# Transposes of the second row tile after a quarter of the first Q tile, and a shorter filler ahead of it

## The chip, the cores and the metric

The kernel runs on one core of a Trainium2 chip. The metric is the time of one execution in device microseconds (us). A profile also gives the span, from the first to the last instruction on the core; it is some 1.7 to 1.9 us shorter than the time. Most tables here are in spans and in moments counted from the span's start, because the change moves a few tenths of a us at one place in the first 8 us.

## The reference

A layer normalization of x (2048 rows of 512), then two branches from the same normalized rows: sliding attention (32 heads of 16, window of 8 with dilation 2) and a gated GELU block of width 1376; the result is x plus both.

```python
x = A_x
xn = _layernorm(x, axis=-1)
return x + _A_ref(xn, A_wqkv, A_wo) + _B_ref(xn, B_w_gate, B_w_up, B_w_down)
# _A_ref begins with: qkv = x @ wqkv     (512 -> 3*512)
# _B_ref: h = gelu(x @ w_gate) * (x @ w_up); h @ w_down
```

What matters for the change is only how the work begins. Before TensorE can do the first product (Q of row tile 0, that is of the first 128 rows), x must land, be normalized by VectorE and ScalarE, be transposed by TensorE into PSUM, and be copied back to SBUF.

## The kernel before

The program is a list of tasks that a small scheduler orders by estimated durations and gives semaphores. The tasks of the start on TensorE (PE) are held in a fixed order by a chain:

```python
WARM = cfg.get("WARM", ([512] * 9 + [128], [512, 128, 128, 128, 128]))
# ... one matmul of ones per entry, to keep the PE busy while it has no data ("fillers")
return lambda e: e.matmul(PS[:, 512 * it.slot:512 * it.slot + wn], lhsT=one_l,
                          rhs=one_r[:, 0:wn], start=True, stop=True)
# ...
if t == 0 and which == 0:                       # Q of row tile 0 is cut in two
    t_mm = G.task("pe", "mma0_0", 8 * 0.0563, mk_mm((0, 1)), ...)    # 8 of its 16 matmuls
    gs = (2, 3)
t_mm = G.task("pe", "mmt%d_%d" % (which, t), 4 * len(gs) * 0.0563, mk_mm(gs), ...)
# ...
chain(warm_tasks[:len(WARM[0])] + ["tpx0_0"] + warm_tasks[len(WARM[0]):] +
      ["mma0_0", "tpx0_1", "mmt0_0", "mmt0_1", "mmt1_0", "tpx1_0", ...])
```

`tpx0_0` and `tpx0_1` are the transposes of row tiles 0 and 1, four matmuls each; `mma0_0` and `mmt0_0` the two parts of Q of tile 0; `mmt0_1` is Q of tile 1, the first that needs tile 1's transposed copy; `mmt1_0` is K of tile 0. The first group of ten fillers stands ahead of tile 0's transposes, the second group of five between them and the first Q matmuls. The fillers are there for PE's clock: its matmuls of 512 columns come 0.427 us apart at first and 0.216 later.

## Time and profile before

| | before |
|---|---|
| time, median of the first 3 runs | 194.46 us |
| span of the profiled run | 192.5 us |
| PE busy | 187.8 us (98%) |
| VectorE, ScalarE busy | 79%, 55% |
| chain that ended last | 95% PE |
| second tile's matmuls wait for the copy | 0.20 us, at 7.47 |

In such a kernel, time is to be had only where PE idles or does work that nobody needs. The fillers are such work, and the 0.20 us such idling; both lie in the first 8 us. The prediction shows the lines.

### The profile page before, as it was taken

Reading aid. Unit: us, or ns where it says so; the run is one execution under the profiler, and the core shown is the slowest. Engines: PE = TensorE matmul, PEld = TensorE weight load, DVE = VectorE, ACT = ScalarE, POOL = GpSimd, SP = SyncE. Lnnn points to the kernel's source line nnn. Section 1 sums busy time; section 2 is a strip of 40 time slices with the busy share of each in tenths; the row PEclk is TensorE's granted clock in tenths of the full one; section 3 lists DMA queues with packets and bytes.
Section 4 is the critical chain, followed back from the end, with each engine's and each line's share of the span. In section 5 each row is a group of like instructions: output and inputs, shape, how many; then the busy total and the mean of one; then the engine's idle time right before and its main releaser. Section 6 shows DMA issues by size and latency. Waiting matters only on the chain.

```text
span 192.5 us, 3287 instructions
## 1 busy us (share of the span) xinstructions
PE 187.8 (98%) x1244; PEld 92.8 (48%) x1260; DVE 151.7 (79%) x239; ACT 105.9 (55%) x176; POOL 15.6 (8%) x31
## 2 busy tenths in 40 slices
PE   8999999999999999999999999999999999999995
PEld 2894444444444444444444444444444444444484
DVE  5799998999999955999698598998996099912132
ACT  5688574686896766700667587338276720058000
POOL 6010011111931100000000000000000000000000
PEclk9999999999999999999999999999999999999999
DMA  4999998799554033984501497510240496130131
GB/s 141 354 393 329 314 183 167 184 280 207 126 127 109 0 90 85 242 190 110 163 0 50 115 243 170 131 64 0 68 144 9 110 232 160 46 112 0 37 87 44
DMA packets 34800, 27.04 MB, mean 140 GB/s; under 512 B 11264, under 2 KB 33248, under 8 KB 34784
## 3 DMA queue, kind: packets, MB, share of 16 engines
q1 hardware_dynamic: 34784, 26.83, 55.9%
q8 instruction: 10, 0.16, 0.3%
q14 instruction: 6, 0.05, 0.1%
HBM read 19.99 MB, written 5.26 MB: 131 GB/s over the span
## 4 chain that ended last, share of the span: by engine, by line
PE 95%; issue 1%; DMA 1%; DVE 0%; ACT 0%; SPq 0%; DVEq 0%
PE PS L1395 36%; PE PS L1474 20%; PE PS L1152 18%; PE PS L1470 7%; PE PS L1363 4%; PE PS L1098 4%; PE PS L1236 4%; PE PS L1430 2%; DMA XIN<-in_A_x_dram 1%; PE PS L1229 1%; PE PS L1040 1%; PE PS L870 0%; SPq L927 0%; DVE XIN L1014 0%; DVE OB L1494 0%
## 5 line engine op out<-in xcount | busy, mean ns | idle before, releaser
L1474 PE MATMUL PS<-Wd,HT 128*128 128x512 bf16 (+2 forms) x208 | 41.1, 345 | 0.1
L1412 ACT ACTIVATE UU<-PS 128x512 bf16<-128x512 f32 x40 | 24.2, 604 | 29.9 <-PE PS L1395 29.8
L1395 PE MATMUL PS<-xnT,Wu 128*128 128x512 bf16 x155 | 39.7, 379 | 0.6 <-issue 0.5
L1395 PE MATMUL PS<-xnT,Wg 128*128 128x512 bf16 x156 | 39.5, 379 | 0.5 <-issue 0.3
L1206 DVE TENSOR_TENSOR UNI<-QT,KT 128x2048 bf16<-128x2048 bf16 x32 | 37.1, 1218 | 2.6 <-PE PS L1363 2.5
L1152 PE MATMUL PS<-xnT,Wqkv 128*128 128x512 bf16 x157 | 35.2, 379 | 0.2
L1405 ACT ACTIVATE GG<-PS 128x512 bf16<-128x512 f32 x40 | 23.8, 602 | 18.9 <-PE PS L1395 15.9
L1417 DVE TENSOR_TENSOR HT<-GG,UU 128x512 bf16<-128x512 bf16 x40 | 16.4, 416 | 18.1 <-ACT UU L1412 18.0
L1474 PEld LDWEIGHTS PS<-Wd,HT 128*128 128x128 bf16 x209 | 19.6, 98 | 18.5
L1395 PEld LDWEIGHTS PS<-xnT,Wu 128*128 128x128 bf16 x160 | 15.4, 98 | 19.4 <-issue 1.3
L1395 PEld LDWEIGHTS PS<-xnT,Wg 128*128 128x128 bf16 x160 | 15.5, 98 | 19.3 <-issue 0.8
L1152 PEld LDWEIGHTS PS<-xnT,Wqkv 128*128 128x128 bf16 x160 | 15.6, 98 | 18.6
L1343 DVE TENSOR_TENSOR UNI<-BS,PT 128x2048 bf16<-128x2048 bf16 x16 | 19.5, 1221 | 1.9 <-DMA out_dram<-OB 1.8
L1343 DVE TENSOR_TENSOR BS<-BS,PT 128x2048 bf16<-128x2048 bf16 x16 | 19.6, 1224 | 0.4
L1494 DVE TENSOR_TENSOR OB<-PS,XR 128x512 bf16<-128x512 f32 (+2 forms) x19 | 11.4, 604 | 10.5 <-PE PS L1474 10.4
L1470 PE MATMUL PS<-Wo,OT 128*128 128x512 bf16 (+2 forms) x75 | 16.9, 345 | 0.1
L1176 ACT ACTIVATE VT<-PS 128x512 bf16<-128x512 f32 x16 | 9.6, 597 | 4.4 <-PE PS L1152 4.4
L944 DVE BATCH_NORM_STATS2 st<-XIN 128x6 f32<-128x512 bf16 x15 | 10.1, 685 | 1.2 <-DMA XIN<-in_A_x_dram 1.2
L1375 ACT ACTIVATE OT<-PS 128x512 bf16<-128x512 f32 x16 | 8.3, 603 | 5.0 <-PE PS L1363 5.0
L1470 PEld LDWEIGHTS PS<-Wo,OT 128*128 128x128 bf16 x76 | 7.2, 98 | 7.0
L1192 POOL COPY KT<-KT 128x64 bf16<-128x64 bf16 x3 | 7.9, 2639 | 15.2 <-ACT KT L1169 13.8
L1162 ACT ACTIVATE QT<-PS 128x512 bf16<-128x512 f32 x12 | 7.2, 597 | 3.1 <-PE PS L1152 3.1
(74 smaller groups left out, 153.0 us busy)
## 6 DMA issues: line engine op xcount, KB each, us to landing
BS<-vt_scratch SPq DMA_DIRECT2D x64, 128.5 KB, 3.5
vt_scratch<-VT SPq DMA_DIRECT2D x16, 128.0 KB
XR<-in_A_x_dram SPq DMA_DIRECT2D x16, 128.0 KB, 3.4
out_dram<-OB SPq DMA_DIRECT2D x14, 128.0 KB, 1.7
Wqkv<-in_A_wqkv_dram SPq DMA_DIRECT2D x3, 512.0 KB
XIN<-in_A_x_dram SPq DMA_DIRECT2D x6, 256.0 KB, 4.3
Wg<-in_B_w_gate_dram SPq DMA_DIRECT2D x1, 1280.0 KB, 8.1
Wu<-in_B_w_up_dram SPq DMA_DIRECT2D x1, 1280.0 KB
```

The lines of the kernel that those rows point to most:

```text
L944: return lambda e: e.bn_stats(out=st[:, t, :], in_=XIN[:, it.slot, t2, :])
L1152: ins = e.matmul(PS[:, 512 * it.slot:512 * it.slot + HWD], lhsT=lhsT, rhs=xnT[:, itx.slot, kt, c0:c0 + HWD], start=(kt == 0), stop=(kt == 3))
L1176: return lambda e: e.activation(out=VT[:, ito.slot, 0:HWD], in_=PS[:, 512 * it.slot:512 * it.slot + HWD], func=ACTF.Identity)
L1206: return lambda e: e.tensor_tensor(out=UNI[:, it.slot, :, :], in0=bass.AP(QT, (itq.slot * 4 + g) * 512, [[NQT * 4 * 512, 128], [0, 4], [1, ...
L1343: return lambda e: e.tensor_tensor(out=dst(), in0=bass.AP(BS, it.slot * 4 * 514 + o, [[NBS * 4 * 514, 128], [514, 4], [128, 4], [1, 128]]) ...
L1395: ins = e.matmul(PS[0:M, 512 * it.slot:512 * it.slot + 512], lhsT=Wx[:, kt, j * 128:j * 128 + M], rhs=xnT[:, itx.slot, kt, :], start=(kt = ...
L1405: return lambda e: e.activation(out=GG[0:M, ito.slot, :], in_=PS[0:M, 512 * it.slot:512 * it.slot + 512], func=ACTF.Gelu_apprx_tanh)
L1412: return lambda e: e.activation(out=UU[0:M, ito.slot, :], in_=PS[0:M, 512 * it.slot:512 * it.slot + 512], func=ACTF.Identity)
L1417: return lambda e: e.tensor_tensor(out=HT[0:M, ito.slot, j, :], in0=GG[0:M, ig.slot, :], in1=UU[0:M, iu.slot, :], op=ALU.mult)
L1470: ins = e.matmul(PS[:, 512 * it.slot:512 * it.slot + CW], lhsT=OT[:, ito.slot, dq, ti * 128:(ti + 1) * 128], rhs=Wo[:, dq, c0:c1], start=( ...
L1474: ins = e.matmul(PS[:, 512 * it.slot:512 * it.slot + CW], lhsT=HT[:, ith.slot, j, ti * 128:(ti + 1) * 128], rhs=Wd[:, j, c0:c1], start=Fal ...
L1494: return lambda e: e.tensor_tensor(out=OB[:, ito.slot, 0:CW], in0=PS[:, 512 * it.slot:512 * it.slot + CW], in1=XR[:, itx.slot, c0:c1], op= ...
```

## The change

The intent is to bring tile 1's transposes, and so its copy, forward, so that the matmuls of tile 1 need not wait for it; and to take out filler that stands in front of the first Q matmuls. The durations that the scheduler plans with are kept, so the order of all other instructions stays.

```diff
-            def mk_w(it=it_warm, wn=wn):
-                return lambda e: e.matmul(PS[:, 512 * it.slot:512 * it.slot + wn], lhsT=one_l,
-                                          rhs=one_r[:, 0:wn], start=True, stop=True)
+            def mk_w(i=i, it=it_warm, wn=wn):
+                n = min(wn, 128) if i >= len(WARM[0]) else wn
+                return lambda e: e.matmul(PS[:, 512 * it.slot:512 * it.slot + n], lhsT=one_l,
+                                          rhs=one_r[:, 0:n], start=True, stop=True)
 ...
-                            t_mm = G.task("pe", "mma0_0", 8 * 0.0563, mk_mm((0, 1)), rd=mrd, wr=[it_mm],
+                            t_mm = G.task("pe", "mma0_0", 8 * 0.0563, mk_mm((0,)), rd=mrd, wr=[it_mm],
 ...
-                            gs = (2, 3)
-                        t_mm = G.task("pe", "mmt%d_%d" % (which, t), 4 * len(gs) * 0.0563, mk_mm(gs), rd=mrd,
+                            gs = (1, 2, 3)
+                        t_mm = G.task("pe", "mmt%d_%d" % (which, t), (8 if len(gs) == 3 else 16) * 0.0563, mk_mm(gs), rd=mrd,
```

Every line number from here on is one higher (L1098 becomes L1099).

## The prediction

> **What bounds the kernel now.** I read the page of the profile first, then the chain of waits cut to the first 20 us, then the timeline of 5 to 8 us, where the changed instructions stand. From the page, the busy table, the slices and the chain:
>
> ```profile
> PE 187.8 (98%) x1244; PEld 92.8 (48%) x1260; DVE 151.7 (79%) x239; ACT 105.9 (55%) x176; POOL 15.6 (8%) x31
> ...
> PE   8999999999999999999999999999999999999995
> ...
> PE 95%; issue 1%; DMA 1%; DVE 0%; ACT 0%; SPq 0%; DVEq 0%
> ```
>
> The reader is to see that TensorE (PE) is the engine at the limit from the first slice to the last, and that the chain that ended last is 95% PE. No other engine can give anything back except at the start, where the chain passes through DMA, VectorE and ScalarE. A tenth of a us taken from a PE gap at the start moves all that follows, if no fixed event (a load that lands when it lands) stands in the way.
>
> The timeline, at the place that is changed (start and length in us):
>
> ```profile
> 5.38 0.95 PE L870 MATMUL PS<-const-bfloat16-1.0 128*128 128x512 bf16 x5
> 5.63 0.38 ACT L1060 ACTIVATE xnT<-PS 128x256 bf16<-128x256 bf16 x1
> ...
> 6.02 0.35 DVE L1014 TENSOR_SCALAR XIN<-XS,rstd 128x512 bf16<-128x512 bf16 x1
> 6.11 0.49 PEld L1098 LDWEIGHTS PS<-xnT,Wqkv 128*128 128x128 bf16 x8
> 6.17 0.61 PE L1098 MATMUL PS<-xnT,Wqkv 128*128 128x128 bf16 x8
> ...
> 6.61 0.39 PE L1040 MATMUL PS<-ident,XIN 128*128 128x128 bf16 x4
> ...
> 6.83 2.60 PE L1098 MATMUL PS<-xnT,Wqkv 128*128 128x128 bf16 x40
> 7.04 0.38 ACT L1060 ACTIVATE xnT<-PS 128x256 bf16<-128x256 bf16 x1 [1.03 <-PE PS L1040]
> ...
> 7.47 1.79 PEld L1098 LDWEIGHTS PS<-xnT,Wqkv 128*128 128x128 bf16 x32 [0.20 <-ACT xnT L1060]
> ```
>
> L870 are the filler matmuls on a constant, L1040 the transposes of a row tile, L1060 the copy of the transposed tile out of PSUM, L1098 the Q and K matmuls. Order on PE: transposes of tile 0, fillers (one of 512 columns, four of 128), 8 Q matmuls of tile 0 (half of its 16), transposes of tile 1, the other 8, then 32 (Q of tile 1, K of tile 0), of which the first need tile 1's copy. The last line is the one that matters: PE stands idle because its next matmul needs tile 1's copy, which ends at 7.04 + 0.38 = 7.42. The 8 matmuls before it have run out at 7.28 (starts at 6.83, one each 0.0555 us), so 0.19 us of PE are lost there. The chain agrees: it goes through the PE queue, not through VectorE:
>
> ```profile
> 5.59 0.74 PE PS L870 x5
> 6.33 0.45 PE PS L1098 x8
> 6.78 0.22 PE PS L1040 x4
> 7.00 0.45 PE PS L1098 x8
> 7.45 0.03 issue
> 7.47 1.96 PE PS L1098 x32
> ```
>
> Tile 1's normalized row is ready at 6.02 + 0.35 = 6.37 (the DVE line), so its transposes, at 6.61, do not wait for data: they stand behind fillers and half a Q tile.
>
> **What the Trainium skill says.** "TensorE: Matmul & The Clock Gate", section "Wait — 56ns, not 53.3ns?", gives start-to-start times of 106.7 and 426.7 ns cold (128 and 512 columns) and 55.6 ns warm (128). The trace agrees: the 512-column filler takes 5.38 to 5.81, 0.43 us; eight Q matmuls go from 6.17 to 6.61, 0.055 us each. The same page, "What's actually happening", has the clock at half rate until a busy window of about 3.4 us has passed, the window not being tied to the kernel's start. Here the trace's clock record goes to full at 6.07 us, in the middle of the fillers, so the fillers are nearly all cold; the page's row of granted clock prints 9 from the start and does not show this. "Perfetto Trace Analysis", section "Tensor Engine Instruction (MATMUL, LD_WEIGHTS)", says that PE ends are estimated; I therefore use starts, and the pitch of 0.0555 us, never the printed 0.22 us of one matmul.
>
> **The change part by part.** The order of instructions on every engine is otherwise the same in both kernels (I compared the two built programs, waits included); the durations that the scheduler plans with were kept, so nothing else is rearranged. Two constants from the trace: a dependent weight load starts 0.05 us after its producer ends (7.42 to 7.47; also 4.92 to 4.97 for tile 0's transposes), and the copy starts 0.26 us after the start of the last transpose (6.78, one pitch before 6.83, to 7.04).
>
> (a) First filler 512 to 128 columns. Removes 0.43 - 0.107 = 0.32 us of filler: five cold ones end at 5.38 + 5 x 0.107 = 5.92. The Q matmuls cannot start there: tile 0's copy ends at 5.63 + 0.38 = 6.01, so the weight load goes at 6.06 and the matmul with it, against 6.17. Worth 0.11 us at that point; 0.14 us of PE idle take the place of the filler.
>
> (b) Four Q matmuls instead of eight ahead of tile 1's transposes. Removes 4 x 0.0555 = 0.22 us in front of them. With (a) the four are done at 6.06 + 0.01 + 4 x 0.0555 = 6.30 (0.01 for the first pair, as between the loads at 7.47 and 7.49). But tile 1 is ready only at 6.37, so the transposes start at 6.43: a new wait of about 0.13 us, and a gain of 6.61 - 6.43 = 0.18 us instead of 0.33.
>
> (c) The copy. Four transposes end at 6.43 + 0.01 + 0.22 = 6.66, the last starting at 6.61; copy from 6.87 to 7.25; the waiting load may go at 7.30, against 7.47.
>
> (d) The 12 matmuls that now stand between: 6.66 + 12 x 0.0555 = 7.33. That is after 7.30, so PE, not the copy, sets the start: the 0.19 us wait is gone, and the 32 matmuls start at 7.33 against 7.48.
>
> Sum: 0.15 us. As a balance of idle time: 0.19 saved at 7.28, 0.32 of filler saved, 0.14 + 0.13 of new waits and small parts given back.
>
> Each part alone, by the same steps: (b) alone has four matmuls from 6.17 to 6.39, the transposes still at 6.43, so the whole 0.15. (a) alone has eight from 6.06 to 6.52, so 0.09. In this reckoning the filler adds nothing once the split is in.
>
> Does 0.15 us reach the end? The next places: tile 2's transposes stand at 9.27 and need its normalization, which ends at 8.71 + 0.35 = 9.06. PE would come at 9.12, the data at 9.11 even unmoved, and the DVE chain that makes it hangs on tile 1's copies and so moves too. K weights are needed at 7.33 + 0.89 = 8.22 and have landed by 7.66, when the gate weights' load, which waits for them, is issued. The gate weights land 8.1 us later, at 15.8, and are used at 16.77. So nothing fixed is in the way. Later PE waits are of 0.2 to 0.4 us behind PE's own results or copies, which move with it. 194.46 - 0.15 = 194.31.
>
> **The rivals.**
> 1. Another wait takes the whole gain: the Q weights. The trace's semaphore updates have them landed at 5.79, 0.27 us before the new start at 6.06, so a late load would cost only the filler's part, and (b) would still get its 0.15. Time 194.3. Against total absorption, 194.46: the slack at tile 2 is thin (0.01 us if DVE does not move), but DVE does move.
> 2. ScalarE becomes the bound: the first Q copy waits for 12 matmuls instead of 8 after the transposes, and starts at 7.53 instead of 7.48, with the small square root of tile 2 behind it. That one also waits for statistics that now come earlier. At most 0.05 us is given back: 194.36.
> 3. The clock: the 0.14 us of idle falls into the window that ends at 6.07. It takes 4% from a window otherwise full of fillers, and a window that began before the fillers was evidently not enough. If that, or the loose phase of the window, kept the clock cold for one more window of 3.4 us, PE would lose 1.7 us: 196.2. The three runs of before are 0.14 us apart, so the phase hardly varies here; I give it 4%.
> 4. Small shifts of DMA and PSUM timing in the remaining 185 us go either way by 0.1 us or so; the spread of before (194.37 to 194.51) is as big as the gain.
>
> **Range and chances.** Middle 194.3. From rivals 2 and 4, 194.0 to 194.6 should hold it 8 times in 10, with the tail above from rival 3. Two per cent is 3.9 us, more than this stretch holds: faster by over 2% has 1%, slower 2%, the same 97%.
>
> **What would show it.** In the changed profile: Q matmuls from about 6.06 in a group of 4; transposes of tile 1 at 6.43 with a wait on VectorE in front of them (the step most likely wrong); copy at 6.87; no wait on ScalarE's copy at 7.3, or under 0.03 us; first gate matmul at 16.62 instead of 16.77; span 192.4. The prediction is wrong if filler or Q matmuls after 6.1 still come 0.107 us apart, if tile 2's transposes wait for VectorE by over 0.1 us, or if the gain at the first gate matmul is not there at the end.

## The result, and the profile after

| | before | after |
|---|---|---|
| median | 194.41 us (6 runs, 193.95 to 194.51) | 194.28 us (6 runs, 194.07 to 194.84) |
| ratio after / before | | 0.9999, 95% interval 0.9983 to 1.0015 |
| span of the profiled run | 192.5 | 192.4 |

A ratio is the mean time of one kernel's fast runs over that of the other's of the same rounds, so it is not quite the ratio of the medians. The measured median is 0.03 us from the predicted 194.31, and inside the range. But the ratio says that the gain of 0.15 us is smaller than what six runs resolve, so the mechanism has to be read from the traces.

The timeline of the changed kernel (start and length in us, engine, line, instruction, count; in brackets the idle time before it and what ended it):

```profile
5.34 0.51 PE L871 MATMUL PS<-const-bfloat16-1.0 128*128 128x128 bf16 x5
5.59 0.39 ACT L1061 ACTIVATE xnT<-PS 128x256 bf16<-128x256 bf16 x1
...
5.98 0.35 DVE L1015 TENSOR_SCALAR XIN<-XS,rstd 128x512 bf16<-128x512 bf16 x1
6.02 0.23 PEld L1099 LDWEIGHTS PS<-xnT,Wqkv 128*128 128x128 bf16 x4 [0.35 <-ACT xnT L1061]
6.03 0.40 PE L1099 MATMUL PS<-xnT,Wqkv 128*128 128x128 bf16 x4 [0.18 <-ACT xnT L1061]
6.39 0.23 PEld L1041 LDWEIGHTS PS<-ident,XIN 128*128 128x128 bf16 x4
6.39 0.40 PE L1041 MATMUL PS<-ident,XIN 128*128 128x128 bf16 x4
6.57 2.50 PEld L1099 LDWEIGHTS PS<-xnT,Wqkv 128*128 128x128 bf16 x44
6.63 2.62 PE L1099 MATMUL PS<-xnT,Wqkv 128*128 128x128 bf16 x44
6.83 0.39 ACT L1061 ACTIVATE xnT<-PS 128x256 bf16<-128x256 bf16 x1 [0.86 <-PE PS L1041]
```

The Q matmuls now wait for the copy of tile 0 (the bracket on L1099) and not for fillers. The transposes stand at 6.39, 0.05 us after tile 1's normalization (5.98 + 0.35 = 6.33). The 44 matmuls after them run in one piece from 6.63 on: the bracket with the wait for the copy, which stood at 7.47 before, is gone.

The chain of waits of the changed kernel at the same place:

```profile
5.59 0.39 ACT xnT L1061
5.98 0.05 issue
6.03 0.40 PE PS L1099 x4
6.42 0.37 PE PS L1041 x4
6.79 2.46 PE PS L1099 x44
9.25 0.22 PE PS L1041 x4
```

Before, this piece of the chain was all PE, with the fillers in it. Now it enters PE from ScalarE's copy, and L871 is no longer in it. The transposes of tile 2 follow at 9.25 against 9.44 before.

From there on nothing differs. Subtracting the moment of the first load of gate weights from the span leaves 175.99 us in the trace before (192.55 - 16.56) and 175.99 in the trace after (192.36 - 16.37). The gain of 0.19 us in the span all arises before 16.4 us, and all of it reaches the end. Of the 0.19, about 0.04 is not the change's: x landed that much earlier in this run (tile 0's normalization ends at 4.89 instead of 4.92). The rest, 0.15, is what the prediction had.

### The profile page after: what moved, and what is told of

Its sections match the earlier page's. It is cut to its first block, busy times and chain, and to the rows that moved or that the text cites. A ratio compares the mean times of both kernels' runs of the same rounds, so it can differ in the third digit from the quotient of the medians.

```text
span 192.4 us, 3303 instructions
## 1 busy us (share of the span) xinstructions
PE 189.0 (98%) x1260; PEld 92.6 (48%) x1260; DVE 151.8 (79%) x239; ACT 105.9 (55%) x176; POOL 15.7 (8%) x31
## 3 DMA queue, kind: packets, MB, share of 16 engines
HBM read 19.99 MB, written 5.26 MB: 131 GB/s over the span
## 4 chain that ended last, share of the span: by engine, by line
PE 96%; DMA 1%; ACT 1%; issue 0%; SPq 0%; DVE 0%; DVEq 0%
PE PS L1396 36%; PE PS L1475 20%; PE PS L1153 18%; PE PS L1471 7%; PE PS L1364 4%; PE PS L1099 4%; PE PS L1237 4%; PE PS L1431 2%; DMA XIN<-in_A_x_dram 1%; PE PS L1230 1%; ACT XR L955 1%; PE PS L1041 0%; SPq L928 0%; ACT xnT L1061 0%; ACT sq L976 0%
## 5 line engine op out<-in xcount | busy, mean ns | idle before, releaser
L1396 PE MATMUL PS<-xnT,Wu 128*128 128x512 bf16 x160 | 40.6, 379 | 0.0
L1396 PE MATMUL PS<-xnT,Wg 128*128 128x512 bf16 x160 | 40.3, 379 | 0.0
L1418 DVE TENSOR_TENSOR HT<-GG,UU 128x512 bf16<-128x512 bf16 x40 | 16.4, 417 | 18.0 <-ACT UU L1413 18.0
```

The source lines that it names most:

```text
L1396: ins = e.matmul(PS[0:M, 512 * it.slot:512 * it.slot + 512], lhsT=Wx[:, kt, j * 128:j * 128 + M], rhs=xnT[:, itx.slot, kt, :], start=(kt = ...
L1418: return lambda e: e.tensor_tensor(out=HT[0:M, ito.slot, j, :], in0=GG[0:M, ig.slot, :], in1=UU[0:M, iu.slot, :], op=ALU.mult)
```

## The experiments

All runs are of one core. By the rule of 2% the verdict of every run is "same", but for e10_lead5_wq_act, which is "unclear"; a run is called slower below where its whole interval lies above 1. Besides the times, each gave a trace. A table of all traces comes first: when the clock goes full (the trace's clock record; "none" where it has no such record), when the last part of the Q weights lands (semaphore updates in the trace), the end of tile 1's normalization, the start of its transposes, the weight load of the first matmul of tile 1 (the point where before had its wait), and the span minus the moment of the first gate weight load.

| run | clock full | Q weights | norm 1 | transposes 1 | first of tile 1 | span | rest |
|---|---|---|---|---|---|---|---|
| before | 6.07 | 5.79 | 6.38 | 6.61 | 7.47 | 192.55 | 175.99 |
| after | 5.45 | 5.56 | 6.34 | 6.39 | 7.26 | 192.36 | 175.99 |
| e1_split_only | 6.31 | 5.81 | 6.30 | 6.46 | 7.32 | 192.42 | 175.99 |
| e2_filler_only | 4.77 | 5.77 | 6.21 | 6.40 | 7.26 | 192.34 | 175.99 |
| e3_lead5 | 5.00 | 5.95 | 6.21 | 6.36 | 7.22 | 192.31 | 176.00 |
| e4_lead12 | 5.10 | 6.15 | 6.19 | 6.95 | 7.81 | 192.89 | 175.99 |
| e5_before_again | 5.64 | 6.55 | 6.35 | 7.13 | 7.99 | 193.10 | 175.99 |
| e7_fill_tiny | none | 5.99 | 6.18 | 6.34 | 7.20 | 192.30 | 175.99 |
| e8_warm_late | 9.72 | 6.19 | 6.30 | 6.71 | 8.31 | 194.10 | 175.98 |
| e9_lead0 | 6.46 | 5.90 | 6.42 | 6.57 | 7.63 | 192.74 | 175.99 |
| e10_lead5_wq_act | 12.88 | 5.26 | 8.57 | 8.77 | 10.26 | 196.62 | 175.98 |
| e11_after_third | 4.86 | 6.01 | 6.17 | 6.37 | 7.22 | 192.32 | 175.99 |
| e12_split_again | none | 5.83 | 6.14 | 6.20 | 7.07 | 192.16 | 175.99 |

The last column is the firmest finding: whatever happens in the first 16 to 21 us, the remaining part takes the same time to within 0.02 us.

Two more things stand in the traces. The clock record runs at full for 187.73 us in nine of them and for 184.32 in e8_warm_late and e10_lead5_wq_act, which is 55 and 54 times 3.413 us: the full clock comes and goes in steps of one such window. And the end of tile 1's normalization moves with the clock: it comes 1.45 us after that of tile 0 where the clock went full after 5.4, and 1.26 to 1.30 us after it where the clock was full by 5.1. Before that normalization VectorE makes its half of tile 0's copy, which waits for PE's transposes of tile 0 (for 0.25 us, until 5.63, in the kernel before). So traces are best compared at like clocks.

### e1_split_only: the long filler with the new split

```diff
-                n = min(wn, 128) if i >= len(WARM[0]) else wn
+                n = wn
```

> The lead of 4 Q matmuls, but the 512-column filler as in the kernel before. Theory (the normalization of tile 1 sets its transposes once the split is in; the filler is then redundant): tile 1's transposes start 0.05 us after its normalization ends, about 1.45 us after tile 0's transposes start, and the first matmul that needs tile 1's copy (second group of L1099 loads) comes as early as in the changed kernel: first gate matmul at about 16.6 us, time 194.3, the same as the changed kernel within 0.05 us of span. Rival (the filler is what mattered): the Q matmuls start at 6.17, all later events keep the old places, first gate matmul at 16.77.

Measured: 194.22 us (5 runs, 194.09 to 194.30), before 194.37 (11 runs), ratio 0.9991 (0.9979 to 1.0002). The timeline:

```profile
5.31 1.06 PE L871 MATMUL PS<-const-bfloat16-1.0 128*128 128x512 bf16 x5
...
6.16 0.47 PE L1099 MATMUL PS<-xnT,Wqkv 128*128 128x128 bf16 x4
6.41 0.27 PEld L1041 LDWEIGHTS PS<-ident,XIN 128*128 128x128 bf16 x4
```

The Q matmuls start at 6.16, as late as in the kernel before, and yet tile 1 comes nearly as early as in the changed kernel (7.32, against 7.26 there and 7.47 before). The rival had tied the later events to the start of the Q matmuls, and falls. The theory holds with one correction: the transposes came 0.16 us after the normalization, not 0.05, because the clock went full late here (6.31), so filler and Q matmuls were still slow. With a late clock the long filler does cost about 0.1 us; it is not fully redundant.

### e2_filler_only: the short filler with the old split

```diff
-                            t_mm = G.task("pe", "mma0_0", 8 * 0.0563, mk_mm((0,)), ...
+                            t_mm = G.task("pe", "mma0_0", 8 * 0.0563, mk_mm((0, 1)), ...
-                            gs = (1, 2, 3)
+                            gs = (2, 3)
```

> Short filler, but 8 Q matmuls ahead of tile 1's transposes as before. Theory: Q matmuls start at about 6.03 to 6.07, the transposes stand behind eight of them (0.45 us later, at 6.5), so tile 1's copy starts 0.09 us earlier than before, and the first gate matmul stands at about 16.68; time 194.37. ScalarE's copy still leaves PE idle for about 0.2 us before the second tile. Rival (filler is the whole effect): first gate matmul at 16.6.

Measured: 194.56 us (6 runs, 194.06 to 194.85), ratio 1.0011 (0.9997 to 1.0024). In its timeline the wait for tile 1's copy is still there, as the theory said:

```profile
5.95 0.62 PE L1099 MATMUL PS<-xnT,Wqkv 128*128 128x128 bf16 x8 [0.26 <-ACT xnT L1061]
...
7.26 1.01 PEld L1099 LDWEIGHTS PS<-xnT,Wqkv 128*128 128x128 bf16 x18 [0.20 <-ACT xnT L1061]
```

The place of the wait (7.26) is earlier than predicted (7.38) because the clock went full at 4.77, before the transposes, which no earlier trace had done. So this run shows which wait remains, but its gain cannot be set against the trace before. The times do not show a gain of the filler at all.

### e3_lead5: one more Q matmul ahead of the transposes

```diff
-                                for g in gs:
-                                    for kt in range(4):
+                                for g, kt in gs:          # gs lists (g, kt) pairs
-  mk_mm((0,)) ... gs = (1, 2, 3)
+  mk_mm(gs[:5]) ... gs = gs[5:]
```

> Short filler and 5 Q matmuls ahead of the transposes (a quarter and one). Theory: the transposes still start when tile 1's normalization is done (the PE idle of 0.13 us before them shrinks to 0.08), and 11 instead of 12 matmuls stand after them, so the next group starts when the copy is done, 0.03 us earlier than in the changed kernel; gain over it 0.03 us of span, not to be seen in the time. Rival (any matmul ahead of the transposes delays them): 0.05 us later than the changed kernel.

Measured: 194.27 us (5 runs, 194.15 to 194.47), ratio 0.9995 (0.9983 to 1.0007); first of tile 1 at 7.22. The expected 0.03 us could not be tested, because another wait took the place of the one that it concerned:

```profile
6.08 0.44 PE L1098 MATMUL PS<-xnT,Wqkv 128*128 128x128 bf16 x5 [0.40 <-DMA Wqkv<-in_A_wqkv_dram]
6.31 0.27 PEld L1041 LDWEIGHTS PS<-ident,XIN 128*128 128x128 bf16 x4
```

The Q matmuls waited for their weights, which landed at 5.95 and not at 5.79, and the transposes then stood behind five matmuls. This is the first rival of the prediction, at work.

### e4_lead12: twelve Q matmuls ahead of the transposes

The edit is that of e3_lead5 with 12 in the place of 5.

> Short filler and 12 Q matmuls ahead of the transposes (three quarters): the change driven the other way. Theory: transposes start 12 x 0.0555 + 0.01 after the Q matmuls' start, at about 6.74; copy at 7.18 to 7.56; only 4 matmuls stand in the gap, so PE is idle for about 0.4 us and the next group starts at 7.6: 0.28 us later than the changed kernel, 0.13 later than before; first gate matmul at about 16.9; time 194.55. Rival (the order is absorbed later): the first gate matmul and the span do not move with it.

Measured: 194.75 us (5 runs, 194.58 to 194.95), ratio 1.0020 (1.0007 to 1.0032): slower, and clear of 1. Waits of PE's weight loads (who waited for whom, us in all, times, longest):

```profile
PEld PS L1098 <- ACT xnT L1061: 1.2, 2, 0.7
```

There are two waits put down to the copies, of 0.7 us for tile 0 (where the Q weights, at 6.15, came later than the copy) and of 0.4 us for tile 1. The first of tile 1 stands at 7.81; 7.6 was expected with weights in time, and they were 0.23 us late for it. This is the change driven the other way: with eight more matmuls ahead of the transposes than in the changed kernel, tile 1 comes 0.55 us later in the trace, part of it from the late weights, and the times are 0.4 us longer. The order matters as the theory says, and its effect reaches the end.

### e5_before_again and e6_after_again: both kernels once more

No edit.

> The kernel before, run again, for a second trace and for the spread of its times. Theory (two things that the kernel does not fix differ from run to run and set the spread: when the clock goes to full, 4.8 to 6.3 us in the six traces so far, and when the Q weights land, 5.6 to 6.2): the ratio to before is 1 within 0.1%, the runs spread by over 0.5 us, and in this trace the first Q matmul starts at the latest of three: fillers over, copy of tile 0 + 0.05, Q weights landed + 0.12. If the clock goes full before 5.4, the long filler ends at 5.7 or so and costs nothing here. Rival (the spread is noise of the chip elsewhere): the parts of the span after the first gate matmul differ between traces by as much as the part before it.

> The changed kernel, run again on the same chip. Theory: 0.05 to 0.2 us below before in the median (ratio 0.9990 to 0.9998), the same spread as before, and from the first gate matmul to the end the same 173.4 us or so as in every other trace. Rival (the change gains nothing, or makes a late clock more frequent): median equal to or above before's.

Measured, e5_before_again: 194.49 us (5 runs, 194.07 to 194.81), ratio of the kernel to itself 0.9998 (0.9985 to 1.0012). Its trace is 0.55 us longer than the first of the same kernel. The chain of waits says why:

```profile
1.71 4.84 DMA Wqkv<-in_A_wqkv_dram
6.55 0.14 issue
6.68 0.61 PE PS L1098 x8
7.29 0.22 PE PS L1040 x4
```

The Q weights landed at 1.71 + 4.84 = 6.55, 0.76 us later than in the first trace, and 0.14 us after that the Q matmuls start. The fillers, over by 6.0 because the clock went full at 5.64, cost nothing here. Expected was an effect of either; this is the larger one. The rival (spread from elsewhere) falls with the last column of the table.

Measured, e6_after_again: 194.30, 194.39, 194.59, and one run, the profiled one, at 404.17 us, which is put down as slow. The three fast runs have a ratio of 1.0002 (0.9988 to 1.0017), and their median, 194.39, is not below before's 194.37: the theory's gain is missed, and in the times the rival has it. (The 173.4 us of the expectation is a slip: from the first gate matmul it is 192.55 - 16.77 = 175.78.) The long run is not an effect of the changed instructions, for it was slow before it reached them. The ten fillers of the first group, which are the same in both kernels, in the timeline of e6_after_again and, below it, of the kernel before:

```profile
0.83 4.44 PE L871 MATMUL PS<-const-bfloat16-1.0 128*128 128x512 bf16 x10 [0.83 <-PEq L1549]
```

```profile
0.83 4.11 PE L870 MATMUL PS<-const-bfloat16-1.0 128*128 128x512 bf16 x10 [0.83 <-PEq L1548]
```

And a later group, from the chains of both, e6_after_again first:

```profile
57.32 16.76 PE PS L1396 x36
```

```profile
30.55 7.77 PE PS L1395 x36
```

That is 0.466 us for a 512-column matmul instead of 0.216, to the end of the run, slower even than the 0.427 of the unwarmed clock elsewhere. It is not that clock either: the Q and K matmuls of this run come 0.056 and 0.166 us apart by turns, where unwarmed ones come a steady 0.107 apart (e8_warm_late). VectorE and ScalarE kept their pace (busy for 155.0 and 107.4 us, against 151.7 and 105.9). What held PE in this one execution is open; it was seen once in the hundred or so runs of all kernels here.

### e7_fill_tiny: almost no filler in the second group

```diff
-                n = min(wn, 128) if i >= len(WARM[0]) else wn
+                n = 1 if i >= len(WARM[0]) else wn
```

> The changed kernel with the five fillers between the transposes and the first Q matmuls cut to 1 column each: PE idle for about 0.6 us there. Theory (the clock window is filled by the first ten fillers; the second group is no longer needed for it, and is not on the path): the clock goes full in the same range of moments, time within 0.1 us of the changed kernel, 194.25. Rival (clock: the idle time keeps the window from counting as busy): the clock goes full up to 3.4 us later in all or some runs, Q and K matmuls come 0.107 us apart, time up to 196.

Measured: 194.02, 195.90, 194.29, 195.80, 194.32 and 194.41 us; ratio 1.0021 (0.9991 to 1.0051). Four runs are as the theory has them and two are 1.6 us longer, as the rival has them. The trace is of the first, a short one, with the clock already full at its transposes:

```profile
4.97 0.40 PE L1041 MATMUL PS<-ident,XIN 128*128 128x128 bf16 x4 [0.38 <-DVE mv L958]
...
6.12 0.38 PE L1099 MATMUL PS<-xnT,Wqkv 128*128 128x128 bf16 x4 [0.65 <-DMA Wqkv<-in_A_wqkv_dram]
```

No trace of a long run was taken. That a late clock is behind the 1.6 us is therefore argued, from the next experiment, and not shown; one window of 3.41 us at half rate would cost 1.7. (The granted clock listed with each run does not tell: e8_warm_late's trace lists 1.000 too, though it was cold until 9.72.) Taken so, the second group of fillers is needed as a guard for the clock, though not for anything on the path.

### e8_warm_late: almost no filler in the first group

```diff
-                n = min(wn, 128) if i >= len(WARM[0]) else wn
+                n = min(wn, 128) if i >= len(WARM[0]) else 8
```

> The changed kernel with the first ten fillers cut to 8 columns each, so that PE does nearly nothing until tile 0's transposes at 4.95: a measure of what a late clock costs. Theory: the clock goes full only after a busy window that begins after 5, between 8 and 12 us; until then Q and K matmuls take 0.107 us instead of 0.0555; 2.3 to 5.5 us at half rate, half of it lost: time 195.4 to 197.0, and the spread between runs well over 0.5 us. Rival (the clock matters little here, the stage waits for normalizations and copies anyway): under 194.8.

Measured: 195.65 us (4 runs, 195.07 to 196.24), ratio 1.0060 (1.0036 to 1.0084). The clock went full at 9.72. The chain of e8_warm_late, to be set against that of the changed kernel above:

```profile
6.33 0.58 PE PS L1099 x4
6.91 0.43 PE PS L1041 x4
7.34 3.65 PE PS L1099 x44
```

The same 44 matmuls take 3.65 us instead of 2.46. A late clock costs over 1 us here, more than anything the change can win; the rival falls.

### e9_lead0: no Q matmul ahead of the transposes

```diff
         G.schedule(SCHED)
+        ma, tx, pe = t_of["mma0_0"], t_of["tpx0_1"], G.order["pe"]
+        # swap the two neighbours (places and planned starts) before semaphores are given
```

A first form, which exchanged the two names in the chain, did not build (the scheduler found no order).

> The changed kernel with no Q matmul ahead of tile 1's transposes (0 instead of 4): the change driven to its end. Theory: the transposes start at tile 1's normalization + 0.06 (6.25 to 6.45, by how early the clock is full), whatever the Q weights do; all 16 Q matmuls of tile 0 stand after them, so the second tile's matmuls start at the later of transposes + 0.23 + 0.89 and weights landed + 0.12 + 0.89, 7.4 to 7.6: up to 0.2 us later than the changed kernel where the weights land before 6.0, earlier where they land after 6.2. PE is idle from the fillers' end to the transposes, about 0.8 us. Time 194.3 to 194.5. Rival (the fewer ahead, the better): second tile's matmuls at 7.25 or before.

Measured: 194.42 us (6 runs, 194.24 to 194.82), before 194.24 (10 runs, one of them at 196.51, which drags the ratio's interval to 0.9957 to 1.0036). The first of tile 1 stands at 7.63, just past the expected 7.4 to 7.6, with the latest clock but two of the table (6.46):

```profile
6.57 0.38 PE L1041 MATMUL PS<-ident,XIN 128*128 128x128 bf16 x4 [0.40 <-DVE XIN L1015]
...
6.79 1.62 PE L1099 MATMUL PS<-xnT,Wqkv 128*128 128x128 bf16 x26
```

PE idles until VectorE has normalized tile 1 and then has all 16 Q matmuls still before it. With e4_lead12 this closes the scan: 0 ahead 7.63, 4 ahead 7.26, 5 ahead 7.22, 12 ahead 7.81, each in its own conditions of clock and weights. By the traces a few matmuls, as many as fit before tile 1 is normalized, are right; the times tell only 12 ahead from the others.

### e10_lead5_wq_act: the Q weights' load on ScalarE's queue

```diff
+            t_w.on_act = nm == "q"        # issued by ScalarE first, at 0.8 us
             t_ld["w" + nm] = t_w
```

on top of e3_lead5: an attempt at a version that beats both, by having the weights always in time.

> 5 Q matmuls ahead of the transposes, and the Q weights' load issued by ScalarE's queue at 0.8 us instead of third on SyncE's at 1.7 us. Theory (late Q weights are what holds the first Q matmul in many runs): the weights land 0.3 to 0.9 us earlier, at 5.0 to 5.5, in time for the copy of tile 0 in every run; no PE wait for the DMA of Wqkv; span 192.3 in this trace and a narrower spread, median 0.1 to 0.2 us below before, 194.2. Rival (the DMA engines are full, the order of issue only moves the wait): tile 1 or tile 0 of x lands later by as much as the weights come earlier, normalizations move from 6.2-6.4 to 6.6 or more, time 194.4 or above.

Measured: 197.80 us (6 runs, 197.16 to 198.35), ratio 1.0168 (1.0129 to 1.0206). The rival is right, and by far more than it said. Waits in its first 9 us:

```profile
ACT XR L956 <- DMA XIN<-in_A_x_dram: 2.8, 1, 2.8
PEld PS L1042 <- DVE XIN L1016: 2.8, 1, 2.8
```

The weights landed at 5.26, but x of tile 1, which ScalarE needs first, became ready for it at 5.62 instead of 3.43, though its load was issued at about 1.25 in both. The Trainium skill, "DMA: Bandwidth & Descriptors", section "Issuing engines are not separate DMA queues", says that loads issued by different engines run on the same 16 DMA engines and interleave, and that issuing from several saves only the sequencer's time; the 2.19 us by which x is later agree. The idle time of PE also put off the clock, to 12.88 us.

### e11_after_third and e12_split_again: more times

No edit to the changed kernel and to e1_split_only.

> The changed kernel for a third time, for a third trace and five more times beside before on one chip. Theory: median 0.05 to 0.15 us below before, no run near 400 us (that state was there from the first filler matmul, 0.44 us or more each instead of 0.43, before any changed instruction), and in the trace 175.98 us from the first gate weight load to the end. Rival (the shorter filler makes a late clock more frequent): at least one of the five over 195.

> The split with the long filler once more, because the times so far do not fit the sum of the two parts: over all fast runs the changed kernel stands level with before (15 runs, mean 194.35, against 32 runs, 194.35, leaving out one of before at 196.51), the filler alone at 194.50 (6 runs), the split alone at 194.20 (5 runs). Theory (the split gives its 0.15 us, and the shortened filler costs about as much in the runs where PE's idle time puts the full clock off): mean 194.2 again, no run over 194.6, 0.1 to 0.2 us below before. Rival (the five runs were lucky; the filler's length does not matter and run-to-run differences of weights and clock hide everything): mean 194.3 to 194.4 with single runs up to 194.8, like the changed kernel.

Measured, e11_after_third: 194.40 us (6 runs, 194.04 to 194.60), before 194.24 (10 runs), ratio 0.9991 (0.9955 to 1.0027); none over 195. The theory's gain is missed again: the median is 0.16 us above before's, not below. It was before that had one long run in this set, 196.51, so the short filler cannot be called the cause of such runs. That run lists a granted clock of 0.991, where before's others list 0.999 or 1.000; by an estimate from these figures, 0.009 x 194.8 x 2, that would be about 3.5 us at half rate. Measured, e12_split_again: 194.42 us (5 runs, 193.88 to 194.64), before 194.33 (9 runs), ratio 1.0006 (0.9992 to 1.0020). Its trace has the shortest span of all, 192.16, and the earliest clock (its fillers go from 0.427 to 0.216 us apart at about 3.6 us), yet its other runs lie where everybody's lie: the rival is right, and the five good runs of e1_split_only were luck.

Taken together, fast runs only and without the 196.51: before has a mean of 194.35 (41 runs), the changed kernel 194.35 (15 runs), the split with the long filler 194.27 (10 runs). A run scatters by 0.2 us (standard deviation), so the means have standard errors of 0.03, 0.06 and 0.07. All 30 runs with four or five Q matmuls ahead (without e7_fill_tiny, e8_warm_late and e10_lead5_wq_act, which change clock or loads) have a mean of 194.31, 0.04 below before, with a standard error of the difference of about 0.05. With the 196.51 left in, before's mean is 194.40. The short filler alone, e2_filler_only, has 194.50, 0.15 above before with a standard error of 0.13: a small cost of the short filler, which would hide a gain of the split, is neither shown nor ruled out.

## Why the prediction was right or wrong

**The bound and the equal rest were right.** PE is the limit to the end, and what is won before the first gate matmul stays won: the rest is 175.98 to 176.00 us in all 13 full-clock traces.

**Step (a), the filler, was right in its place and only conditional in its worth.** In the trace after, the Q matmuls start 0.05 us after the copy of tile 0, at 6.03. But its worth of 0.11 us at that point holds only if the clock is late and the Q weights are early. In e5_before_again the fillers were over by 6.0 and the weights were not there until 6.55, so the filler cost nothing. Nor does the prediction's balance of idle time close: 0.19 + 0.32 - 0.14 - 0.13 is 0.24 and not 0.15, and the 0.09 left to "small parts" is mostly filler that it counted as cold. In the trace before, the clock went full during the last fillers, so all five took 0.79 us (5.38 to 6.17) and not 0.43 + 4 x 0.107 = 0.85.

**Steps (b), (c) and (d) were right to 0.04 us.** Predicted were transposes at 6.43, the copy from 6.87 to 7.25, the first of tile 1 at 7.33 with no wait. The trace has 6.39, 6.83 to 7.22, and 7.30 for that matmul, all earlier by the 0.04 us by which x was earlier. The new wait in front of the transposes, called the step most likely wrong, is there (four Q matmuls from 6.03 end at 6.26, the transposes start at 6.39: 0.13 us, as predicted).

**"(b) alone the whole 0.15" was nearly right.** e1_split_only has the gain with the old start of the Q matmuls; e2_filler_only keeps the wait for the copy. With the late clock of e1_split_only's trace the filler added 0.1 us in front of the transposes.

**Rival 1 was understated.** The prediction took the landing of the Q weights, 5.79, for a fixed fact with 0.27 us of slack. It was one draw from 5.56 to 6.55 (the traces with the load on its old queue and the full clock). In seven of those twelve traces the Q matmuls start 0.13 or 0.14 us after the landing, so the weights are more often the last to come than the copy or the fillers are. When they bind, the split still gains: from the trace of e5_before_again, four instead of eight matmuls from 6.69 would put the transposes at 6.69 + 4 x 0.0555 = 6.91 and the first of tile 1 at 6.91 + 16 x 0.0555 = 7.80 instead of 7.99. This is an estimate of 0.19 us, not a run.

**Rival 2 did not come.** In the trace after, the first copy of Q on ScalarE starts at 7.50, against 7.48 before, and PE does not wait for it.

**Rival 3 rested on a wrong step:** "The three runs of before are 0.14 us apart, so the phase hardly varies here". Three runs were too few. The moment of the full clock runs from 4.77 to 6.46 in the traces with a record that keep the first fillers and x on its queue, and the times of one and the same kernel from 193.95 to 194.81, with one at 196.51. No shift of the clock by a whole window was seen in a trace of the changed kernel, apart from the run at 404 us, which is another thing.

**The size in the times stays open.** The one pair of traces that could be put on a level, before and after, gives 0.15 us, the pooled times 0.00 (standard error 0.06) for the changed kernel and 0.04 (0.05) for all kernels with the split. These times do not contradict a gain of 0.1 us, they sit badly with 0.15 in every run, and they do not show a gain. The middle of 194.31 agrees with the measured 194.28 in part by luck, since the scatter of a median of six runs is as large as the gain. The range, 194.0 to 194.6, and the 97% for "same" were sound. A likely reason for a smaller mean gain is that the traces are of the first run of each set, and that clock, weights and x fall otherwise in the following ones; that was not shown.

## What to carry to other kernels

When the engine at the limit waits for a chain that passes through itself (transpose, copy, matmul), put only as many other matmuls ahead of the transpose as fit before its input is ready; the last wait of the chain, here the normalization of the second tile, tells how many. Filler that keeps the clock up may not be free to cut, even where it is off the path: with almost none of the second group, two runs of six were 1.6 us longer, ten times what the cut could win, and a late clock is the likely cause, though not shown. And before a gain of 0.1% is believed or dismissed, compare the part of the span behind the change, which here is equal to 0.02 us, and look at what differs from run to run ahead of it.

## What the Trainium skill lacked or had wrong

- "TensorE: Matmul & The Clock Gate", section "What's actually happening", says that the moment of the full clock varies by 500 ns either way. Here it ran from 4.77 to 6.46 us in the nine traces with a clock record in which PE began at 0.83 us and was kept busy (and was at about 3.6 us in e12_split_again, by the pitch of its fillers), and to 9.72 and 12.88 us where it was left idle.
- The same page has the two states of half and full rate and, in section "Seeing it yourself", a lasting quarter rate and a limit of 13/16. One whole execution here fits none of them: 0.466 us for a 512-column matmul over 402.5 us of span, against 0.427 unwarmed and 0.216 warm, 128-column matmuls 0.056 and 0.166 us apart by turns, and its first fillers already slow (4.44 us for ten, against 4.11).
- No page that I read has how much the landing of one load differs between runs of one program: 512 KB issued at 1.71 to 1.73 us landed between 5.56 and 6.55 us.
- No page that I read has the time from the end of a producer's copy to the start of the waiting weight load; it is 0.05 us in these traces (7.42 to 7.47 before).
